# Attention mix on one core: output weights split a round after their loads, fewer single maxima at units' first steps, and the order of the second scores

## The chip, the cores and the metric

The kernel runs on one core of one Trainium2 chip. The metric is device time in microseconds (us). Before the change, three runs took 1511.3 us in the median (1510.62 to 1514.53).

## The reference

Two attention branches over the same input of 2048 positions and 512 features are mixed by a gate for each position. Branch A is a local, dilated attention (32 heads of 16, eight keys, two apart). Branch B is full attention with 32 query heads and one shared key and value head.

```python
g = sigmoid((x * gate_w).sum(-1, keepdims=True))
a = A(x, wqkv, wo_a)      # softmax over 8 keys at distance 0, 2, ..., 14
b = B(x, wq, wk, wv, wo_b)  # softmax(q k^T / 4) v, all 2048 keys, k and v shared by 32 heads
out = g * a + (1 - g) * b
```

All is float32. The weights wq and wk of branch B are drawn eight times as large as the others, so the softmax needs its row maximum.

## The kernel before

**Stages.** Until about 270 us the projections run (`stream` over `lumps`), and with them the first part of the row maxima. Then the main loop runs 512 steps, `s` from 0 to 511, and one more for what is left. A step belongs to unit `u = s // 16` (four heads and 512 queries; 32 units) and key tile `kt = s % 16` (128 keys).

**One step.** It issues, in the order of `order`: the scores of two heads and their exponential (`exp_pair(s, 0)`: two matmuls on the lower and upper 64 rows of the array into bank `eb[0]`, one ScalarE activation over 1024 columns); a pair of row maxima for a later unit (`fill_pair` into `m2`: two matmuls, one VectorE reduction over both); a single maximum (`fill_one` into `m1`: one matmul on one half of the array, one VectorE reduction); the scores and the exponential of the other two heads (`exp_pair(s, 1)`); and the weighted sums of the step before (`weighted(s - 1)`, into `po`). In a unit's first step (`kt == 0`) the sums of the unit just ended are complete: `finish_a` transposes `po` on VectorE (L497) and takes reciprocals.

**The maxima.** Each unit needs 64 halves (one matmul and its maximum each); a pair makes two, a single one. They leave `slots` in a fixed order; a single takes half of a slot, lower rows (`odd` 0) first, and leaves the other in `half`. The planner keeps a clock for each engine (`clk`) and the time at which each bank is free (`free`), from fixed costs: `T_R` 0.23, `T_EXP` 0.92, `T_RED2` 1.14, `T_RED1` 0.61, `T_W` 1.21 us. `fill_ready` issues a pair if `m2` will be free within `M2S` = 0.5 us, a single if `m1` will within `M1S` = 0.3 us. `singles(s)` asks whether pairs alone would be too few for what is to go:

```python
return 2 * max(0, 16 * (NU - 1) - 16 - s) + PER_ROW * max(0, NJ - 4 - outs) < to_go()
```

If a unit's maxima are still missing when its start is near, `pause` issues pairs one after the other on the banks `e0`, `e1` and `m2`, ahead of the step's scores. It is asked for when fewer than two steps are left before the due time (six steps ahead of the unit), for what is missing less 2.8 per step.

**The output.** Three phases (`out_phase`, in units 14, 18 and 25) multiply four rows of tiles by the output weights, and make maxima meanwhile; one begins when branch A is far enough and the lead of the maxima is under `LEAD` = 3 units. The last four rows are made by `spread`, four pairs of matmuls to a step, from the time at which at most nine halves are to go.

**Branch A and the output weights.** Branch A runs on GpSimd, as a list of pieces (`work`), two groups to a round; `run_pool` issues pieces while their planned time is less than 2.5 us ahead. The output weights, eight pieces of 128 x 512, are loaded by SyncE (`wo_load`, L625) into one of two buffers and split into a rounded high part (ScalarE copy, L81) and the rest (GpSimd subtraction, L82). Each round of the first five in the main loop takes two entries of `wos`, and an entry holds the load of one piece and the split of the one before. ScalarE works its instructions in their order, so what stands behind a split waits with it.

Of the kernel before, what the change touches and what calls it, by code (L numbers as in the profile page):

```python
# [19 lines left out]
C = D // P  # L20
# [4 lines left out]
NU = NQB * NHG  # L25
# [23 lines left out]
def gated_mix_kernel(ctx, tc, xt, wa, wk, wq, wo_a, wo_b, out):  # L49
# [20 lines left out]
    def home(v):  # L70

        return (v % NB, v - NB) if v < 2 * NB - 2 else ((v - NB) % (NB - 2), v - NB + 2)
# [11 lines left out]
    clk = {"pe": 0.0, "act": 0.0, "dve": 0.0}  # L84

    def after(eng, ready, dur):
        clk[eng] = max(clk[eng], ready) + dur
        return clk[eng]
# [213 lines left out]
    half = []  # L302
    free = {"m2": 0.0, "m1": 0.0, "e0": 0.0, "e1": 0.0, "po": 0.0}
    tasks, shifted, pm = [], set(), []
# [21 lines left out]
    def to_go():  # L326
        return 2 * len(slots) + len(half)
# [137 lines left out]

    pe, pexp, exped = [], {}, {}

    def exp_pair(s, pr, other=False):
        bank, key = (m2, "m2") if other else (eb[pr], f"e{pr}")
        u, kt = divmod(s, NJ)  # L470
        for odd in range(2):
            b = 64 * odd
            nc.tensor.matmul(bank[:, odd, :], kst[b:b + 64, kt * P:(kt + 1) * P], qst[home(u)[0]][b:b + 64, pr, :], start=True, stop=True)  # L473
        e = px.tile([P, 2, 512], F32, name="pexp", bufs=6)
        nc.scalar.activation(e, bank, AF.Exp, scale=SCALE)  # L475
        free[key] = after("act", after("pe", free[key], T_R) + T_LAT, T_EXP)
        exped[s] = free[key]
        pexp[s, pr] = e
# [50 lines left out]
    def a_load(g, hf):  # L529
        e = wp.tile([P, HALO + NH, AN], F32, name="aext", bufs=2)  # L530
        src = ad[g]
        nc.gpsimd.dma_start(e.rearrange("p r n -> p (r n)"), bass.AP(tensor=src.tensor, offset=src.offset + NH * hf * AN, ap=[[NJ * AN, P], [1, (HALO + NH) * AN]]))
        aext[g] = e
# [33 lines left out]
    def a_sub(g):  # L567
        lgv = alog[g].rearrange("p w j h -> p w (j h)")
        nc.gpsimd.tensor_sub(lgv, lgv, amx.pop(g).unsqueeze(1).to_broadcast([P, W, NH * AG]))
# [10 lines left out]
    def a_add_up(g):  # L580

        lgv = alog[g].rearrange("p w j h -> p w (j h)")
        half = p2[0].tile([P, W // 2, NH * AG], F32, name="half", tag="tr2", bufs=1)
        asum[g] = p2[0].tile([P, NH, AG], F32, name="asum", bufs=2)
        nc.gpsimd.tensor_add(half, lgv[:, 0:4], lgv[:, 4:8])
        nc.gpsimd.tensor_add(half[:, 0:2], half[:, 0:2], half[:, 2:4])
        nc.gpsimd.tensor_add(asum[g].rearrange("p j h -> p (j h)"), half[:, 0], half[:, 1])
# [19 lines left out]
    p2b = []  # L607
# [15 lines left out]
    def wo_load(k, c):  # L623
        wot[k, c] = p2b[0].tile([P, 512], F32, name="os", tag="two", bufs=2)
        nc.sync.dma_start(wot[k, c], (wo_a, wo_b)[k][c * P:(c + 1) * P, :])  # L625

    def wo_split(k, c):
        t = wot.pop((k, c))
        split(woh[k][:, c, :], wol[k][:, c, :], t, nc.gpsimd)
# [219 lines left out]
    later_rows, spread_at, row_left = [], [0.0], [0]  # L849

    def singles(s):

        return 2 * max(0, 16 * (NU - 1) - 16 - s) + PER_ROW * max(0, NJ - 4 - outs) < to_go()
# [86 lines left out]

    wos = []
    kcs = [(k, c) for k in range(2) for c in range(C)]
    for i in range(2 * C + 1):
        wos.append([(wo_load, kcs[i])] if i < 2 * C else [])
        wos[-1] += [(wo_split, kcs[i - 1])] if i else []

    def work():

        def sub(g, hf):
            yield lambda: ("max", g, hf) in done  # L950
            a_sub(g)
            hooks.append((pool + 3000, a_exp, g, ("exp", g, hf)))
            yield 500
            summing.append((g, hf))

        def sums():

            if summing and ("exp",) + summing[0] in done:
                g, hf = summing.pop(0)
                a_add_up(g)  # L960
                hooks.append((pool + 800, a_sum, g, ("sum", g, hf)))
                yield 800

        def values(g, hf):
            while ("sum", g, hf) not in done:
                if summing:
                    yield lambda: ("exp",) + summing[0] in done
                    yield from sums()
                else:
                    yield lambda: ("sum", g, hf) in done  # L970
            yield lambda: g < 8 or p2b
            yield from a_values(g, hf)
            if g == NAG - 1:
                done.add(hf)

        def load(i):
            if i < len(order):
                yield lambda: order[i][0] // GC < ready_gg
                a_load(*order[i])
                yield 600 if i else 6200  # L980

        order = [(g, hf) for hf in range(2) for g in range(NAG)]
        extra, summing = list(wos), []
        yield from load(0)
        yield from load(1)
        for i in range(0, len(order), 2):
            yield from a_scores(*order[i])
            hooks.append((pool + 3500, a_max, order[i][0], ("max",) + order[i]))
            for k, x in enumerate(a_scores(*order[i + 1])):
                yield x  # L990
                if k == 6:
                    yield from sub(*order[i])
                if k == 11:
                    yield from sums()
            hooks.append((pool + 3500, a_max, order[i + 1][0], ("max",) + order[i + 1]))
            for k, x in enumerate(values(*order[i])):
                yield x
                if k == 6:
                    yield from sub(*order[i + 1])
                if k == 11:  # L1000
                    yield from sums()
            yield from load(i + 2)
            yield from values(*order[i + 1])
            yield from load(i + 3)
            for _ in range(2):
                if p2b and extra:
                    for f, a in extra.pop(0):
                        f(*a)
                    yield 1300
        assert not extra  # L1010

    pieces, blocked = [work()], []

    def run_pool():
# [93 lines left out]
    for s in range(NS + 1):  # L1108
        u, kt = divmod(s, NJ)
        if s == 16 * NB + 4:  # L1110
            half_back()
        if len(stacked) < NU and s > 16 * (home(len(stacked))[1] + 1):
            stack(len(stacked))
        if s < NS and kt == 0 and u not in shifted:
            while u not in shifted:
                clk["pe"] += 0.5
                run_tasks()
                if u not in shifted and left.get(u, 1):
                    assert pause(4)
        v = min(x[0][0] for x in (half, slots, [(NU,)]) if x)  # L1120
        need = left.get(v, NF // NU)
        steps = 16 * v - 6 - s
        short = need - 2.8 * max(0, steps) if v < NU else 0
        lead = (NF - to_go()) / 64 - s / 16
        order = (0, "m2", "m1", 1) if s > 1 else (1, "m2", 0, "m1") if s else ()
        k, n = outs // 4, C - (outs >= NJ - 4)
        if outs == NJ - 4:
            if NU - 3 in shaped and to_go() <= 9 and not later_rows and "last" not in done:
                later_rows.append(spread(list(range(outs, NJ)), n))
            if short > 0 and steps < 2:  # L1130
                pause(short)
        elif due or outs < NJ and s and kt == 0 and outs // NH in done and NHG * (k + 1) - 1 in shaped and (lead < LEAD or s >= 16 * (NHG * (k + 2) + 1)):
            if not due:
                prepare(outs, n)
                due.append(n)
            else:
                out_phase(list(range(outs, outs + 4)), due.pop(), kt == 1)
                outs += 4
                order = (0, "m1", 2)
        elif short > 0 and steps < 2:  # L1140
            pause(short)

        for which in order:
            if which == "m2":
                fill_ready("m2", M2S)
            elif which == "m1":
                if not later_rows and singles(s):
                    fill_ready("m1", M1S)
            elif s < NS:
                exp_pair(s, which % 2 or which // 2, which == 2)  # L1150
        spread_some(4)
        if s:
            weighted(s - 1)
            if kt == 0 and s < NS:
                finish_a(u - 1, nc.gpsimd)
        run_tasks()
        run_pool()
# [64 lines left out]
```

## Time and profile before

| | us |
|---|---|
| median of three runs | 1511.3 |
| profiled execution, device time | 1510.97 |
| its span, first to last instruction | 1509.2 |
| TensorE (PE) busy | 1484.5 (98%) |
| ScalarE (ACT) busy | 1280.1 (85%) |
| VectorE (DVE) busy | 1193.7 (79%) |
| GpSimd (POOL) busy | 1021.5 (68%) |

In the rows, a group shows its line, engine, operation, and `out<-in` by the program's names, then the count, the busy time, the mean duration in ns, and the idle time before it with what ended it. PEld is the weight load of TensorE, which overlaps its matmuls (PE). A row of the timeline begins with its start and its length. In a windows row the length, the busy times with counts, TensorE's granted clock (1.00 is full), the DMA share and GB/s follow one another. The tile `pexp` is an exponential, `pe` a bank of scores, `pm` is `m2`, `ps` is `m1`, `mx` holds maxima, `os` a loaded piece of the output weights and `woh` its high part.

### The profile page before, as it was taken

The numbers are of one execution on the slowest core, as the hardware profiler recorded it, in microseconds if no ns is written. First come the engines' busy times: TensorE is split into PE (matmuls) and PEld (weight loads), VectorE is DVE, ScalarE is ACT, GpSimd is POOL, SyncE is SP. The second block draws the span as 40 slices with busy tenths as digits, with TensorE's granted clock in tenths as the row PEclk, the third lists the DMA queues.
The fourth block names the chain that finished last, engine by engine and source line by source line (L and its number), as shares of the span: only waits on it lengthen the run. The fifth ranks groups of instructions, "written<-read, shape, count | busy, mean of one in ns | idle before, by whom it ended". The sixth has DMA issues, their size and how long they took to land.

```text
span 1509.2 us, 29437 instructions
## 1 busy us (share of the span) xinstructions
PE 1484.5 (98%) x11020; PEld 710.6 (47%) x11020; DVE 1193.7 (79%) x1822; ACT 1280.1 (85%) x1660; POOL 1021.5 (68%) x1804
## 2 busy tenths in 40 slices
PE   9999999999989999999999999999999999999998
PEld 6998988433333333333363334633333363333343
DVE  6966666788878888888888888888888888888812
ACT  5468977899979999999988998899989978998975
POOL 7866988787878889888888789888888040111020
PEclk9999999999999999999999999999999999999999
DMA  6744233121120211211202102021120010000000
GB/s 218 216 146 138 78 102 98 33 83 56 49 84 1 83 58 41 69 40 41 69 27 76 48 30 79 30 70 44 37 69 12 12 33 19 2 2 2 1 1 28
DMA packets 44287, 87.75 MB, mean 58 GB/s; under 512 B 9520, under 2 KB 25952, under 8 KB 39920
## 3 DMA queue, kind: packets, MB, share of 16 engines
q1 hardware_dynamic: 37136, 46.89, 10.3%
q0 software_dynamic: 6432, 37.94, 7.5%
q8 instruction: 86, 1.41, 0.4%
q10 hardware_dynamic: 576, 1.05, 0.2%
q14 instruction: 57, 0.47, 0.1%
HBM read 59.02 MB, written 26.30 MB: 57 GB/s over the span
## 4 chain that ended last, share of the span: by engine, by line
PE 88%; ACT 5%; POOL 2%; DVE 2%; issue 2%; DMA 1%; SPq 0%; DVEq 0%; ACTq 0%; POOLq 0%
PE po L483 32%; PE pe L473 25%; PE pm L324 8%; PE pe L1059 6%; PE ps L324 4%; PE pe L740 4%; PE pm L409 2%; ACT pexp L475 2%; ACT dd L419 2%; PE pm L812 1%; PE ps L409 1%; PE po L409 1%; POOL qlo L220 1%; POOL qraw L213 1%; PE pe L183 1%
## 5 line engine op out<-in xcount | busy, mean ns | idle before, releaser
L475 ACT ACTIVATE pexp<-pe 128x1024 f32<-128x1024 f32 x1021 | 989.5, 1022 | 110.0 <-PE pe L473 105.8
L344 DVE TENSOR_REDUCE mx<-pm 128x2 f32<-128x1024 f32 x506 | 618.0, 1221 | 150.0 <-PE pm L324 147.8
L483 PE MATMUL po<-pexp,vst 128*32 128x512 f32 x4096 | 546.5, 605 | 1.1 <-DVE tt L497 0.7
L473 PE MATMUL pe<-qst,kst 64*128 64x512 f32 x1914 | 532.9, 455 | 7.4 <-ACT pexp L475 7.2
L473 PEld LDWEIGHTS pe<-qst,kst 64*128 64x128 f32 x1914 | 219.8, 185 | 414.4 <-ACT pexp L475 404.8
L355 DVE TENSOR_REDUCE mx<-ps 128x1 f32<-128x512 f32 x473 | 321.4, 680 | 4.1 <-PE ps L324 4.1
L324 PE MATMUL pm<-kst,qst 62*128 62x512 f32 x964 | 199.9, 404 | 1.4 <-ACT pexp L475 0.8
L324 PE MATMUL ps<-kst,qst 62*128 62x512 f32 x447 | 189.2, 423 | 0.5 <-DVE mx L355 0.3
L543 POOL TENSOR_TENSOR pr<-aext 128x256 f32<-128x256 f32 x256 | 182.3, 737 | 2.8 <-ACT dd L419 2.6
L603 POOL TENSOR_TENSOR oa<-oa,av 128x256 f32<-128x256 f32 x224 | 164.0, 732 | 15.0
L483 PEld LDWEIGHTS po<-pexp,vst 128*32 128x32 f32 x4096 | 80.9, 108 | 185.6 <-issue 173.1
L600 POOL TENSOR_TENSOR av<-aext,lg 128x256 f32<-128x256 f32 x224 | 139.3, 622 | 12.7
L509 POOL TENSOR_TENSOR rl<-rl,gate_t 128x16 f32<-128x16 f32 x31 | 6.8, 221 | 175.0 <-DVE rl L503 174.9
L324 PEld LDWEIGHTS ps<-kst,qst 62*128 62x128 f32 x447 | 82.4, 184 | 77.0 <-DVE mx L355 74.2
L1059 PE MATMUL pe<-wah,xl 64*128 64x384 f32 (+1 forms) x504 | 107.8, 338 | 0.0
L1059 PE MATMUL pe<-wah,xh 64*128 64x384 f32 (+1 forms) x504 | 107.5, 338 | 0.2 <-ACT gate L253 0.2
L1059 PE MATMUL pe<-wal,xh 64*128 64x384 f32 (+1 forms) x504 | 107.5, 337 | 0.0
L419 ACT ACTIVATE dd<-pm 128x512 f32<-128x512 f32 x164 | 90.8, 610 | 17.8 <-PE pm L409 10.8
L429 DVE CUSTOM_DVE_ANT_0 dd<-ps,dd 128x512 f32<-128x512 f32 x82 | 56.7, 692 | 59.5 <-ACT dd L419 29.0
L324 PEld LDWEIGHTS pm<-kst,qst 62*128 62x128 f32 x964 | 94.7, 188 | 9.5 <-DVE mx L344 4.3
L549 POOL TENSOR_TENSOR tr<-pr 128x512 f32<-128x512 f32 x64 | 81.6, 1275 | 3.7
L549 POOL TENSOR_TENSOR tr<-tr 128x256 f32<-128x256 f32 (+1 forms) x128 | 72.5, 566 | 8.7
(214 smaller groups left out, 1902.6 us busy)
## 6 DMA issues: line engine op xcount, KB each, us to landing
aext<-ad POOLq DMA_DIRECT2D x32, 1056.0 KB, 5.5
ad<-stage SPq DMA_DIRECT2D x32, 384.0 KB
qst<-qd SPq DMA_DIRECT2D x60, 128.0 KB
xraw<-xt SPq DMA_DIRECT2D x16, 256.0 KB
qd<-qhi SPq DMA_DIRECT2D x16, 256.0 KB
qd<-qlo SPq DMA_DIRECT2D x16, 256.0 KB
qst<-qd SPq DMA_DIRECT2D x60, 64.0 KB
qst<-ml SPq DMA_DIRECT2D x216, 2.0 KB
```

Of the source, the lines that this page charges most:

```text
L324: nc.tensor.matmul(dst, qst[home(v)[0]][b:b + 62, pr, t * P:(t + 1) * P], kst[b:b + 62, kc * 512:(kc + 1) * 512], start=True, stop=True)
L344: nc.vector.tensor_reduce(m[:, :, pr, t, kc], dst, AX.X, ALU.max)
L355: nc.vector.tensor_reduce(m[:, odd, pr, t, kc:kc + 1], dst, AX.X, ALU.max)
L419: nc.scalar.activation(dd[0][:, odd], m2[:, odd, :], AF.Abs)
L473: nc.tensor.matmul(bank[:, odd, :], kst[b:b + 64, kt * P:(kt + 1) * P], qst[home(u)[0]][b:b + 64, pr, :], start=True, stop=True)
L475: nc.scalar.activation(e, bank, AF.Exp, scale=SCALE)
L483: nc.tensor.matmul(po[32 * i:32 * i + 32, :], vst[:, kt, :], pexp[s, i // 2][:, i % 2, :], start=(kt == 0), stop=(kt == NJ - 1))
L543: nc.gpsimd.tensor_mul(pr[:, k], q, e[:, o:o + NH, AC:2 * AC])
L549: nc.gpsimd.tensor_add(nx, cur[:, :, 0:n], cur[:, :, n:2 * n])
L600: nc.gpsimd.tensor_mul(av, e[:, o:o + NH, 2 * AC:].rearrange("p j (h d) -> p j h d", d=DH), lg[:, w].unsqueeze(3).to_broadcast([P, NH, AG, ...
L603: nc.gpsimd.tensor_add(ao, ao, av)
L1059: nc.tensor.matmul(front[2 if x == last else x % 2][0][:, b, :n], l[h], r[h], start=(i == 0), stop=(i == 3 * C - 1))
```

## The change

Four edits. The scores of a pair can be issued upper rows first; the second pair of a step does so when the half left in `half` is an upper one, that is, when a single has just used the lower rows. A single is not issued in a unit's first step, except in unit 0's and in the last eight units. A round's entry of `wos` now splits two pieces, those loaded in the round before, and asks for two loads, which the planner issues at 5 us later on its clock. A round takes one entry, charged as 2600 ns of GpSimd, instead of two of 1300.

```diff
-    def exp_pair(s, pr, other=False):
+    def exp_pair(s, pr, other=False, first=0):
...
-        for odd in range(2):
+        for odd in (first, 1 - first):
...
+    def wo_soon(k, c):
+        tasks.append((clk["pe"] + 5.0, wo_load, (k, c)))
...
-    for i in range(2 * C + 1):
-        wos.append([(wo_load, kcs[i])] if i < 2 * C else [])
-        wos[-1] += [(wo_split, kcs[i - 1])] if i else []
+    for i in range(0, 2 * C + 2, 2):
+        wos.append([(wo_split, x) for x in kcs[i - 2:i]] if i else [])
+        wos[-1] += [(wo_soon, x) for x in kcs[i:i + 2]]
...
-            for _ in range(2):
-                if p2b and extra:
-                    for f, a in extra.pop(0):
-                        f(*a)
-                    yield 1300
+            if p2b and extra:
+                for f, a in extra.pop(0):
+                    f(*a)
+                yield 2600
...
+        first = 0
         for which in order:
...
-                if not later_rows and singles(s):
+                if not later_rows and (kt or not s or u >= NU - 8) and singles(s):
+                    first = half[0][4] if half else 0
                     fill_ready("m1", M1S)
             elif s < NS:
-                exp_pair(s, which % 2 or which // 2, which == 2)
+                exp_pair(s, which % 2 or which // 2, which == 2, first)
```

## The prediction

> **What bounds the kernel now.** I read the page first, then the waits, the timeline of the steady loop, the windows around the one long stall, and the counts of the two kinds of maximum.
>
> ```profile
> span 1509.2 us, 29437 instructions
> PE 1484.5 (98%) x11020; PEld 710.6 (47%) x11020; DVE 1193.7 (79%) x1822; ACT 1280.1 (85%) x1660; POOL 1021.5 (68%) x1804
> PE 88%; ACT 5%; POOL 2%; DVE 2%; issue 2%; DMA 1%; SPq 0%; DVEq 0%; ACTq 0%; POOLq 0%
> L475 ACT ACTIVATE pexp<-pe 128x1024 f32<-128x1024 f32 x1021 | 989.5, 1022 | 110.0 <-PE pe L473 105.8
> L344 DVE TENSOR_REDUCE mx<-pm 128x2 f32<-128x1024 f32 x506 | 618.0, 1221 | 150.0 <-PE pm L324 147.8
> ```
>
> TensorE (PE) is busy 98% of the span and holds 88% of the chain that ended last. ScalarE's two exponentials of a step (about 1.0 us each) wait 105.8 us in all for PE, and VectorE's pair reductions 147.8 us. So the loop of 512 steps is paced by PE, with ScalarE close behind. How close shows in a step without a single, read from the weight loads of the scores (a step runs from one such row with an idle time of 0.84 to the next):
>
> ```profile
> 1335.40 0.19 PEld L473 LDWEIGHTS pe<-qst,kst 64*128 64x128 f32 x2 [0.84 <-ACT pexp L475]
> 1337.30 0.19 PEld L473 LDWEIGHTS pe<-qst,kst 64*128 64x128 f32 x2 [0.84 <-ACT pexp L475]
> 1339.48 0.19 PEld L473 LDWEIGHTS pe<-qst,kst 64*128 64x128 f32 x2 [0.84 <-ACT pexp L475]
> 1341.66 0.19 PEld L473 LDWEIGHTS pe<-qst,kst 64*128 64x128 f32 x2 [0.84 <-ACT pexp L475]
> ```
>
> The first step has no single and takes 1.90 us, the next two have one and take 2.18 each.
>
> **Part one, the output weights.**
>
> ```profile
> L81 ACT ACTIVATE woh<-os x8: 629/632/634, 318.6 to 568.6; 128x512 fp32r<-128x512 f32 x8
> ACT woh L81 <- DMA os<-wo_b: 4.4, 1, 4.4
> 446.14 0.63 ACT L81 ACTIVATE woh<-os 128x512 fp32r<-128x512 f32 x1 [4.38 <-DMA os<-wo_b]
> 411.29 0.70 DVE L497 STREAM_TRANSPOSE tt<-po 128x512 f32<-128x512 f32 x1
> 451.74 0.72 DVE L497 STREAM_TRANSPOSE tt<-po 128x512 f32<-128x512 f32 x1 [0.92 <-PE po L483]
> 487.01 0.71 DVE L497 STREAM_TRANSPOSE tt<-po 128x512 f32<-128x512 f32 x1
> 521.41 0.71 DVE L497 STREAM_TRANSPOSE tt<-po 128x512 f32<-128x512 f32 x1
> 447.00:450.00 3.00, 2.27 (x11) 1.45 (x15) 1.00 (x1) 2.78 (x4) 3.00 (x4) 0.50 0.02 5
> 450.00:453.00 3.00, 3.00 (x14) 1.16 (x7) 1.93 (x5) 1.37 (x2) 2.33 (x4) 0.50 0.00 0
> ```
>
> Of the eight splits' copies on ScalarE exactly one waits for its load, 4.38 us; queued behind it are the exponentials, and behind those PE. The transposes (L497) come once a unit: 40.45 us, 35.27 us, and 34.40 for the unit after. So the stall with what follows it costs 40.45 + 35.27 - 2 x 34.40 = 6.9 us, more than the wait, because TensorE's granted clock is 0.50 for some 6 us afterwards (the windows' column after the engines). Changed, each split follows its load by a whole round, some 62 us (the copies lie between 318.6 and 568.6 in four rounds' time), so nothing waits. What is late next is ScalarE itself: two copies of 0.63 us now stand together in four rounds. Such a pair exists already:
>
> ```profile
> 504.06 1.94 ACT L475 ACTIVATE pexp<-pe 128x1024 f32<-128x1024 f32 x2 [0.26 <-PE pe L473]
> 507.99 1.15 ACT L81 ACTIVATE woh<-os 128x512 fp32r<-128x512 f32 x2
> 513.05 1.94 ACT L475 ACTIVATE pexp<-pe 128x1024 f32<-128x1024 f32 x2 [0.26 <-PE pe L473]
> ```
>
> Four steps from 504.06 to 513.05 take 8.99 against 4 x 2.15 (34.40 / 16) = 8.60: 0.4 for a pair. The stalled round becomes such a pair (0.4 stays), the last round gains a second copy (0.2). Part one: -6.9 + 0.4 + 0.2 = **-6.3 us**, between -4.4 (the wait alone) and -6.9. GpSimd's two subtractions of a round stay as they are, charged 2600 ns where they had 2 x 1300. On SyncE's queue the loads come 5 us of planned time later, behind whatever strips of maxima and queries were put there meanwhile; those belong to units well ahead, and the loads have a round to spare. They reuse the buffers of the splits just made, which GpSimd has read by then. Nothing.
>
> **Part two, no single at the first steps of units 1 to 23.** Each unit now issues about 15 singles and skips one at its third step, where VectorE is late from the finishing of the previous unit:
>
> ```profile
> 867.53 0.19 PEld L473 LDWEIGHTS pe<-qst,kst 64*128 64x128 f32 x2 [0.84 <-ACT pexp L475]
> 867.88 0.19 PEld L324 LDWEIGHTS pm<-kst,qst 62*128 62x128 f32 x2 [0.16 <-DVE mx L344]
> 869.54 0.19 PEld L473 LDWEIGHTS pe<-qst,kst 64*128 64x128 f32 x2 [0.84 <-ACT pexp L475]
> 1346.60:1381.00 34.40, 10.21 (x15) 1.00 0.00 1
> 1346.60:1381.00 34.40, 19.56 (x16) 1.00 0.00 1
> 1415.70:1459.00 43.30, 3.41 (x5) 1.00 0.01 1
> 1415.70:1459.00 43.30, 9.74 (x8) 1.00 0.01 1
> ```
>
> (The window rows count the reductions of singles, then of pairs: the first two in unit 28, the last two from the start of unit 30 to its end.) The step with the skip takes 2.01, so one with a single (34.40 - 2.01) / 15 = 2.16. Does the planner put the lost single back at the third step? By its own costs, no. There m2 is what it waits for, and m1 comes free T_RED1 = 0.61 after m2, while PE has moved on by T_R = 0.23: 0.38 late, where M1S allows 0.3. The chain that sets this starts with the finishing of the unit, in both kernels. So the first step is a second skip: 23 x (2.16 - 1.90) = **-6.0 us**, between -3.5 (if the new skip costs 2.01 like the old) and -7.
>
> But the 23 halves (single maxima) remain to be done, and `singles` is true wherever I work it out (a unit makes 15 + 2 x 16 = 47 halves, so at step 464, where the rule's threshold is 32, some 68 are to go), so every place for a single is already taken and nothing later takes them up. They arrive at unit 30. Today 2 x 8 + 5 = 21 halves are left there, and they end at step 488 of 512. Changed, 44 are left. Nine steps (480 to 488) issue three each, but two at the third: 26. At step 489 the rule of `pause` applies (one step before the due time of unit 31): 18 left, less 2.8, is 15.2, so eight pairs are issued in a row on e0, e1 and m2, ahead of the exponentials. Their price is VectorE's:
>
> ```profile
> 1423.46 0.19 PEld L473 LDWEIGHTS pe<-qst,kst 64*128 64x128 f32 x2 [0.84 <-ACT pexp L475]
> 1424.24 1.23 DVE L344 TENSOR_REDUCE mx<-pm 128x2 f32<-128x1024 f32 x1 [0.29 <-PE pm L324]
> 1425.38 0.68 DVE L355 TENSOR_REDUCE mx<-ps 128x1 f32<-128x512 f32 x1
> 1425.66 0.19 PEld L473 LDWEIGHTS pe<-qst,kst 64*128 64x128 f32 x2 [0.84 <-ACT pexp L475]
> ```
>
> The reductions of step 488 end 2.60 after its start (1426.06 - 1423.46); the pairs follow at 1.22 each (the mean of L344), and the seventh frees e0, for which the first scores of step 489 wait: 2.60 + 7 x 1.22 = 11.1, instead of 2.20. That is 8.9 us in which ScalarE has nothing to do and PE little. The other seven of the 23 halves are issued in ordinary steps, four of them as singles in steps 485 to 488, which have none today: 4 x 0.26 = 1.0. Together **+9.9 us**, between +4 (half as many pairs, if the planner finds places) and +14 (three pairs more).
>
> The last four rows of the output, spread four pairs of matmuls to a step, start five steps later as well. What covers that:
>
> ```profile
> L812 PE MATMUL pm<-woh,own x48: 387/393/502, 1434.1 to 1481.7; 64*128 64x512 f32 x48
> L812 PE MATMUL pm<-woh,turned x64: 387/392/396, 1439.6 to 1487.8; 64*128 64x512 f32 x64
> 1486.26 0.30 PEld L473 LDWEIGHTS pe<-qst,kst 64*128 64x128 f32 x4 [0.84 <-ACT pexp L475]
> 1489.09 0.30 PEld L473 LDWEIGHTS pe<-qst,kst 64*128 64x128 f32 x4 [0.84 <-ACT pexp L475]
> 1497.53 0.16 PEld L483 LDWEIGHTS po<-pexp,vst 128*32 128x32 f32 x8 [1.26 <-ACT pexp L475]
> ```
>
> They run from 1434.1 to 1487.8, twenty steps; from 1489.09 to the last weighted sum at 1497.53 there are four steps without them. Those take the delayed rows, and the very last step the rest. With that cover gone, a step's worth costs 2.83 (1486.26 to 1489.09) - 1.90 = 0.9. The output phases that wait for the lead to fall below LEAD may begin a unit earlier (a dozen halves are 0.2 of a unit's 64), with the same work: nothing.
>
> **Part three, the order of the second scores.** A step puts seven matmuls on the two halves of the array: two, two, one, two. The half that has the single runs four, the other three, in either order. Before the change every second single leaves with the half that the next scores begin with, the others with the opposite one, and the two steps of 2.18 above are one of each. So **0**, within 0.01 x some 225 such steps = 2 us either way.
>
> **The sum.** -6.3 - 6.0 + 9.9 + 0 = -2.4 us. The profiled run took 1510.97 (1.8 around its span); less 2.4 it is 1508.6. The median of the three runs is 0.3 higher, so I forecast 1511.3 - 2.4 = **1508.9 us**.
>
> **The rivals.**
>
> *A: the single is moved, not lost.* If m1 is planned to be free in time at the third step, that step gets the single that the first one loses. Then nothing is left over at unit 30, and each unit gains 2.01 - 1.90 = 0.11: 1511.3 - 6.3 - 23 x 0.11 = 1502.5. It needs the 0.38 to shrink below 0.3; what else is charged to PE's plan there could do that, the unchanged chain speaks against it.
>
> *B: the order of the halves counts.* If a single in the half that goes first did cost time, the steps with it would be the longer ones. 0.05 on 225 of them would be 11 us: 1508.9 - 11 = 1498. The equal steps speak against it.
>
> *C: the catch-up ends slower.* One mechanism, at step 489: the halves left there. If VectorE's lateness takes a second single from each of the 23 units (at the fourth step, where m1 is then more than 0.3 late as well), 11.5 more pairs cost 14.0, less 23 x 0.26 = 6.0 saved on the way: +8.0, 1516.9. It decides from about 20 halves more (+7, over the bound below); the 15 singles of unit 28, one skip for its finishing, speak against it. PE's clock would add to it:
>
> ```profile
> 447.73 0.29 PEld L473 LDWEIGHTS pe<-qst,kst 64*128 64x128 f32 x2 [5.22 <-ACT pexp L475]
> 454.57 0.19 PEld L473 LDWEIGHTS pe<-qst,kst 64*128 64x128 f32 x2 [0.84 <-issue]
> SPq L461 <- POOL ml L447: 246.8, 16, 46.8
> ```
>
> After the stall two steps took 6.84 instead of 4.30 at a clock of 0.50: 2.5 us more. In the catch-up PE is not idle but has two matmuls every 1.22 us; whether that keeps the clock, this trace does not show, so 2.5 stands in the range. The Trainium skill (TensorE: Matmul & The Clock Gate, Part 1: The HAM clock gate) says that after an idle window of about 3.4 us the array runs at half its clock until it has been busy for such a window. By that rule, with the sparse pairs counted as idle, the catch-up would cost 12.4 instead of 9.9 and the sum be +0.1; the trace agrees with the rule after the idle 5 us, where it granted 0.50.
>
> *D: the splits still wait.* SyncE's strips wait up to 46.8 us for GpSimd (the last row); loads behind such a wait come late. A wait as long as a round would put the 6.3 back: 1508.9 + 6.3 = 1515.2. Rounds of 62 us speak against it.
>
> **How the numbers follow.** The forecast's case has 0.6, A 0.13, B 0.07, C 0.14, D 0.06. The forecast's own range is 1504 to 1513.5, from the bounds of its terms, the catch-up's above all. A is inside the range that I give, B is left out; above, it reaches to C's middle: 1502 to 1516.5. A run tells a change from none at about 0.3%, 4.5 us: under 1506.8 or over 1515.8. Faster: A and B and a tenth of the forecast's case, 0.26. Slower: most of C, little of D, 0.15. Within: 0.59.
>
> **What would show it.** The wait of L81 for a load is gone, and no stretch at clock 0.50 near 450 us; between transposes 34.1 to 34.2 us where it was 34.4; L355 some 15 to 20 fewer, and in unit 30 a row of eight pair reductions without exponentials beside them, with scores waiting 9 us for VectorE; L812 starting 15 to 20 us later. Wrong would be: singles at third steps (A), steps that shorten by 0.05 all along (B), more than twelve pairs in that row (C), an L81 that still waits (D).

## The result and the profile after

The changed kernel takes 1501.03 us in the median of four runs (1498.46 to 1501.06), the kernel before 1510.96 beside it: a ratio of 0.9925, with 95% between 0.9907 and 0.9944. In a later comparison it was 0.9907 [0.9891, 0.9923]. So the change brings 0.6 to 1.1%. The forecast was 1508.9 with a range from 1502.0; the result lies 1 us below that range, on the side of faster, where most of the chance had been put on no difference that can be told.

The page of the kernel after (profiled execution 1498.46 us):

```profile
span 1496.7 us, 29437 instructions
PE 1477.2 (99%) x11020; PEld 711.1 (48%) x11020; DVE 1192.2 (80%) x1815; ACT 1281.0 (86%) x1664; POOL 1025.9 (69%) x1808
PE 89%; ACT 4%; POOL 3%; issue 2%; DVE 1%; DMA 1%; SPq 0%; DVEq 0%; POOLq 0%; ACTq 0%
L344 DVE TENSOR_REDUCE mx<-pm 128x2 f32<-128x1024 f32 x512 | 625.0, 1221 | 145.5 <-PE pm L324 142.2
L355 DVE TENSOR_REDUCE mx<-ps 128x1 f32<-128x512 f32 x455 | 309.4, 680 | 3.2 <-PE ps L324 3.2
```

PE bounds the kernel as before. The pair reductions (L344) went from 506 to 512. The totals don't say where 12.5 us of the span went; for that the span is cut in three at the transposes of line L497, of which one comes at the start of each unit. The group of the thirty that begin units 1 to 30, before and after:

```profile
L497 DVE STREAM_TRANSPOSE tt<-po x30: 705/707/717, 308.1 to 1417.6; 128x512 f32<-128x512 f32 x30
```

```profile
L497 DVE STREAM_TRANSPOSE tt<-po x30: 701/717/720, 307.3 to 1403.1; 128x512 f32<-128x512 f32 x30
```

The first start is called the lead-in, from it to the last start is the way (units 1 to 29), and the rest of the span is the end (units 30 and 31, with the catch-up). Before: 308.1, 1109.5 and 91.6. After: 307.3, 1095.8 and 93.6. So the way is 13.7 us shorter and the end 2.0 longer. All runs cut in this manner:

| kernel | lead-in | way | end | against the kernel before, 95% |
|---|---|---|---|---|
| before | 308.1 | 1109.5 | 91.6 | |
| after | 307.3 | 1095.8 | 93.6 | 0.9925 [0.9907, 0.9944] |
| e1_weights | 310.4 | 1102.7 | 91.9 | 0.997 [0.996, 0.998] |
| e2_order | 313.2 | 1107.9 | 91.5 | 1.0003 [0.9993, 1.0013] |
| e3_singles | 310.0 | 1103.0 | 93.6 | 0.9975 [0.9966, 0.9984] |
| e4_no_order | 309.4 | 1095.6 | 93.6 | 0.9927 [0.9914, 0.9941] |
| e5_all_units | 311.5 | 1093.6 | 97.4 | 0.9934 [0.9922, 0.9947] |
| e6_due_later | 309.1 | 1095.7 | 93.0 | 0.9921 [0.9907, 0.9934] |
| e7_sixth_step | 310.8 | 1098.1 | 92.5 | 0.9929 [0.9915, 0.9942] |
| e8_two_skips | 309.3 | 1093.8 | 105.7 | 0.9997 [0.9988, 1.0006] |
| e9_split_singly | 310.9 | 1095.9 | 93.6 | 0.993 [0.9915, 0.9945] |
| e10_singly_due_later | 310.0 | 1095.8 | 93.0 | 0.9912 [0.9896, 0.9927] |
| e11_all_units_later | 309.4 | 1093.6 | 98.1 | 0.9927 [0.9911, 0.9943] |
| e12_changed_again | 310.9 | 1095.8 | 93.6 | 0.9907 [0.9891, 0.9923] |

The lead-in, which the edits hardly touch, differs by up to 5.9 us from one execution to the next. The way and the end of the same program (after and e12) agree to 0.1 us. Where the stall is still there the way is less steady: the split's wait is 4.4 us in the trace of before, 4.2 in that of e2 and 5.5 in that of e3, and e2's way is 1.6 us shorter than before's with no difference in its ratio. So single terms of a microsecond or two are read from the way and the end of kernels without the stall, and whether a kernel as a whole is faster from the ratios.

Now the prediction's lines. The output weights after: the group of the copies, ScalarE's timeline at the former stall, and the window around it (length, busy times with counts, granted clock, DMA share, GB/s):

```profile
L81 ACT ACTIVATE woh<-os x8: 629/632/636, 377.3 to 559.7; 128x512 fp32r<-128x512 f32 x8
435.94 1.94 ACT L475 ACTIVATE pexp<-pe 128x1024 f32<-128x1024 f32 x2 [0.19 <-PE pe L473]
437.77 1.15 ACT L81 ACTIVATE woh<-os 128x512 fp32r<-128x512 f32 x2
438.81 5.95 ACT L475 ACTIVATE pexp<-pe 128x1024 f32<-128x1024 f32 x6
430.00:450.00 20.00, 19.84 (x141) 7.03 (x141) 16.71 (x19) 18.89 (x22) 18.50 (x31) 1.00 0.31 103
```

The copies stand in pairs and wait for nothing, the exponentials follow without a gap, and the clock stays at 1.00 where it had been 0.50.

The first steps, by the weight loads of the scores at the start of unit 7:

```profile
510.35 0.18 PEld L473 LDWEIGHTS pe<-q,kst 64*128 64x128 f32 x2 [0.84 <-ACT pexp L475]
512.25 0.19 PEld L473 LDWEIGHTS pe<-q,kst 64*128 64x128 f32 x2 [0.84 <-ACT pexp L475]
514.38 0.19 PEld L473 LDWEIGHTS pe<-q,kst 64*128 64x128 f32 x2 [0.84 <-ACT pexp L475]
514.53 0.19 PEld L324 LDWEIGHTS pm<-kst,qst 62*128 62x128 f32 x2
516.27 0.19 PEld L473 LDWEIGHTS pe<-q,kst 64*128 64x128 f32 x2 [0.84 <-ACT pexp L475]
```

The first step takes 1.90, as forecast. The third, still without a single, takes 1.89; it was 2.01 before. Its pair (514.53) follows the scores with no wait for VectorE, where before it waited 0.16 us for the reduction of the pair ahead (at 867.88). That was not forecast.

The end: the reductions of singles, then of pairs, from the start of unit 30 to that of unit 31, and PE's loads, VectorE and the window at the catch-up:

```profile
1401.60:1443.50 41.90, 4.76 (x7) 1.00 0.01 1
1401.60:1443.50 41.90, 14.30 (x12) 1.00 0.01 1
1419.52 0.19 PEld L324 LDWEIGHTS pe<-kst,qst 62*128 62x128 f32 x2 [0.84 <-ACT pexp L475]
1420.13 1.23 DVE L344 TENSOR_REDUCE mx<-pe 128x2 f32<-128x1024 f32 x1 [0.51 <-PE pe L324]
1421.28 1.22 DVE L344 TENSOR_REDUCE mx<-pm 128x2 f32<-128x1024 f32 x1
1421.41 0.30 PEld L473 LDWEIGHTS pe<-qst,kst 64*128 64x128 f32 x4 [1.55 <-DVE mx L344]
1423.66 0.19 PEld L324 LDWEIGHTS pm<-kst,qst 62*128 62x128 f32 x2 [0.84 <-issue]
1417.00:1423.00 6.00, 4.84 (x38) 1.86 (x34) 4.65 (x5) 4.41 (x7) 0.99 (x1) 1.00 0.02 4
```

7 + 2 x 12 = 31 halves were left at unit 30, not 44. At step 489 two pairs stand in a row, not eight; the scores wait 1.55 us for VectorE, the step takes 4.14 us (1419.52 to 1423.66), and the clock stays at 1.00.

### The profile page after: what moved, and what is told of

Read it like the earlier page. It is cut to its first block, busy times and chain, and to the rows that moved or that the text cites. A ratio compares the mean times of both kernels' runs of the same rounds, so it can differ in the third digit from the quotient of the medians.

```text
span 1496.7 us, 29437 instructions
## 1 busy us (share of the span) xinstructions
PE 1477.2 (99%) x11020; PEld 711.1 (48%) x11020; DVE 1192.2 (80%) x1815; ACT 1281.0 (86%) x1664; POOL 1025.9 (69%) x1808
## 4 chain that ended last, share of the span: by engine, by line
PE 89%; ACT 4%; POOL 3%; issue 2%; DVE 1%; DMA 1%; SPq 0%; DVEq 0%; POOLq 0%; ACTq 0%
PE po L483 34%; PE pe L473 25%; PE pm L324 8%; PE pe L1061 6%; PE ps L324 5%; PE pe L743 4%; PE pm L409 2%; PE pm L815 1%; ACT dd L419 1%; PE ps L409 1%; POOL qlo L220 1%; PE po L409 1%; POOL qraw L213 1%; ACT pexp L475 1%; PE pe L183 1%
## 5 line engine op out<-in xcount | busy, mean ns | idle before, releaser
L344 DVE TENSOR_REDUCE mx<-pm 128x2 f32<-128x1024 f32 x512 | 625.0, 1221 | 145.5 <-PE pm L324 142.2
L473 PE MATMUL pe<-qst,kst 64*128 64x512 f32 x1914 | 522.8, 454 | 3.8 <-ACT pexp L475 2.6
L473 PEld LDWEIGHTS pe<-qst,kst 64*128 64x128 f32 x1914 | 214.5, 184 | 417.0 <-ACT pexp L475 406.6
L355 DVE TENSOR_REDUCE mx<-ps 128x1 f32<-128x512 f32 x455 | 309.4, 680 | 3.2 <-PE ps L324 3.2
L324 PE MATMUL ps<-kst,qst 62*128 62x512 f32 x429 | 180.6, 421 | 0.7 <-DVE mx L429 0.4
L324 PEld LDWEIGHTS ps<-kst,qst 62*128 62x128 f32 x429 | 78.8, 184 | 71.6 <-DVE mx L355 66.6
```

The lines of the kernel that those rows point to most:

```text
L324: nc.tensor.matmul(dst, qst[home(v)[0]][b:b + 62, pr, t * P:(t + 1) * P], kst[b:b + 62, kc * 512:(kc + 1) * 512], start=True, stop=True)
L344: nc.vector.tensor_reduce(m[:, :, pr, t, kc], dst, AX.X, ALU.max)
L355: nc.vector.tensor_reduce(m[:, odd, pr, t, kc:kc + 1], dst, AX.X, ALU.max)
```

## The experiments

### One part at a time

Three kernels are the kernel before with one part of the change each. **e1_weights** has the edit of `wos` and `work` alone:

```diff
...
-    for i in range(2 * C + 1):
-        wos.append([(wo_load, kcs[i])] if i < 2 * C else [])
-        wos[-1] += [(wo_split, kcs[i - 1])] if i else []
+    for i in range(0, 2 * C + 2, 2):
+        wos.append([(wo_split, x) for x in kcs[i - 2:i]] if i else [])
+        wos[-1] += [(wo_soon, x) for x in kcs[i:i + 2]]
...
```

> The kernel before with the output weights' edit alone. My theory: the one wait of a split for its load (4.38 us) goes, and with it the half-clock stretch behind it, less about 0.6 for copies standing in pairs: -6.3 us, and no L81 that waits for a load. Rival (the wait only moves, because the loads reach their buffers late behind SyncE's other waits): within 2 us of before, with an L81 that still waits.

```profile
L497 DVE STREAM_TRANSPOSE tt<-po x30: 704/705/707, 310.4 to 1413.1; 128x512 f32<-128x512 f32 x30
```

The way is 1102.7, 6.8 shorter than before, and the end 0.3 longer: -6.5 where -6.3 was forecast. No copy of L81 waits for a load. The ratio of the whole gives less, 4.5 us with 3.0 to 6.0. The -6.5 is from one trace of each kernel and lies just outside that interval; the lead-in, 2.3 us longer in this trace, is in the whole, and the stall of the kernel before is not the same in every run.

**e2_order** has `first` alone:

```diff
...
-        for odd in range(2):
+        for odd in (first, 1 - first):
...
```

> The kernel before with the order of the second scores alone. My theory: seven matmuls on halves of the array, four on the half with the single in either order: 0, within 2 us. Rival (a single in the half that goes first costs time): -11 us, 0.05 on each of some 225 steps; a weaker form of it, -3 us, is what would be left of the whole change's -9.9 after -6.3 for the weights if the singles' edit gave nothing.

The ratio is 1.0003 [0.9993, 1.0013]. The order is worth nothing that can be told, or at most 2 us either way by that interval.

**e3_singles** has the rule on singles alone:

```diff
-                if not later_rows and singles(s):
+                if not later_rows and (kt or not s or u >= NU - 8) and singles(s):
```

> The kernel before with the rule for singles alone. As predicted: -6.0 on the way and +9.9 at unit 30, so +3.9 us. What the changed kernel's trace suggests instead: some -8 on the way (23 first steps at 1.90, and third steps at 1.90 where they were 2.01) and +2 at the end, so -6 us, with about 30 halves left at unit 30's start instead of 44, because units with an even count of singles make a full pair where before a lone half took the pair's bank, and because output phases hold 36 sums instead of 34.

```profile
L497 DVE STREAM_TRANSPOSE tt<-po x30: 699/716/718, 310.0 to 1413.0; 128x512 f32<-128x512 f32 x30
ACT woh L81 <- DMA os<-wo_b: 5.5, 1, 5.5
```

The way is 6.5 shorter than before, although the one wait for a load is now 5.5 us where it was 4.4. The end is 2.0 longer, as in the kernel after: -4.5 in all, where -6 was expected once the trace of the changed kernel was known. So the two effective parts add up: 6.8 + 6.5 = 13.3 of 13.7 on the way, 0.3 + 2.0 at the end.

**e4_no_order** is the kernel after with the order taken out, a second look at it where no stall disturbs it:

```diff
-                    first = half[0][4] if half else 0
+                    first = 0
```

> The changed kernel with the old order of the second scores (lower rows always first). My theory: as the changed kernel, 1501 us, within 2. Rival (the order gives what is missing): 1504 to 1512 us.

The way is 1095.6 against 1095.8, the end the same. The order does nothing.

### Why the skipped single gains on the way

**e7_sixth_step** leaves as many places out, but each unit's sixth step instead of its first:

```diff
-                if not later_rows and (kt or not s or u >= NU - 8) and singles(s):
+                if not later_rows and (kt != 5 or u == 0 or u >= NU - 8) and singles(s):
```

> The changed kernel with the single left out at the sixth step of units 1 to 23 instead of the first. If it counts only that a unit has one single fewer (an even number, so that pairs are kept whole, and 0.26 us less of PE): units 1 to 29 as much shorter as with the first step, but for the third step, which goes back to 2.00 (+2.3 us in all); the lone halves in m2's place stay at two or fewer. If the first step itself is what matters (the finishing of the unit before then meets a free VectorE): the sixth step's gain is eaten elsewhere, and the stretch of units 1 to 29 is some 7 us longer than the changed kernel's, as in the kernel with the weights' edit alone.

The steps of a unit by the loads of the scores (the unit starts at 858.21; the row of its fifth step is left out):

```profile
L497 DVE STREAM_TRANSPOSE tt<-po x30: 704/706/708, 310.8 to 1408.9; 128x512 f32<-128x512 f32 x30
858.21 0.19 PEld L473 LDWEIGHTS pe<-qst,kst 64*128 64x128 f32 x2 [0.84 <-ACT pexp L475]
860.35 0.18 PEld L473 LDWEIGHTS pe<-qst,kst 64*128 64x128 f32 x2 [0.84 <-ACT pexp L475]
862.53 0.19 PEld L473 LDWEIGHTS pe<-qst,kst 64*128 64x128 f32 x2 [0.84 <-ACT pexp L475]
864.52 0.18 PEld L473 LDWEIGHTS pe<-qst,kst 64*128 64x128 f32 x2 [0.84 <-ACT pexp L475]
...
868.82 0.19 PEld L473 LDWEIGHTS pe<-qst,kst 64*128 64x128 f32 x2 [0.84 <-ACT pexp L475]
870.72 0.19 PEld L473 LDWEIGHTS pe<-qst,kst 64*128 64x128 f32 x2 [0.84 <-ACT pexp L475]
```

The sixth step takes 1.90, and the third is back at 1.99. The way is 1098.1: 4.6 less than with the weights alone (1102.7), 2.3 more than after. So of the 6.9 us that the rule on singles gives after the weights, 4.6 come from any single left out in a unit, and 2.3 from its being the first step's. Most of the second number is the third steps': 1.99 against 1.89 in the units shown, some 2 us in the 21 units whose first step lost its single and that hold no output phase. After a first step without a single VectorE has done with the finishing of the unit in time for the third step's pair. One thing expected here didn't come: 6 lone halves still took the pair's bank (units 1 to 29), where two or fewer had been forecast.

### How much may be skipped

**e8_two_skips** leaves out the first and the ninth step, so that the catch-up must come:

```diff
-                if not later_rows and (kt or not s or u >= NU - 8) and singles(s):
+                if not later_rows and (kt not in (0, 8) or u == 0 or u >= NU - 8) and singles(s):
```

> The changed kernel with singles left out at the ninth step as well as the first, units 1 to 23. This is the prediction's rival C on purpose: the halves are really missing now, and the planner issues about ten pairs in a row before unit 31 and three or so before unit 30. At 1.22 us a pair (eleven more than in the changed kernel) that is +13.4, less 22 x 0.26 = 5.7 on the way: +7.7, some 1508.7 us. If PE's clock falls in the catch-up: 2.5 to 5 more. If pairs in a row are cheap (0.23 us of PE each): -3.

The counts of unit 30 as above, then the catch-up: PE, VectorE and ScalarE, and three windows, the first of them around a smaller catch-up before unit 30:

```profile
1401.60:1454.20 52.60, 5.44 (x8) 0.90 0.01 1
1401.60:1454.20 52.60, 23.36 (x20) 0.90 0.01 1
1423.96 0.50 PE L324 MATMUL pe<-kst,qst 62*128 62x512 f32 x2 [0.63 <-DVE mx L344]
1424.95 1.21 DVE L344 TENSOR_REDUCE mx<-pm 128x2 f32<-128x1024 f32 x1
1425.09 0.76 PE L324 MATMUL pe<-kst,qst 62*128 62x512 f32 x2 [0.63 <-DVE mx L344]
1426.09 2.34 DVE L344 TENSOR_REDUCE mx<-pe 128x2 f32<-128x1024 f32 x2
1432.77 1.94 ACT L475 ACTIVATE pexp<-pe 128x1024 f32<-128x1024 f32 x2 [12.59 <-PE pe L473]
1382.00:1388.00 6.00, 3.54 (x25) 1.40 (x23) 4.66 (x5) 2.56 (x3) 0.00 (x0) 1.00 0.00 0
1419.00:1425.00 6.00, 3.28 (x20) 1.04 (x12) 5.82 (x7) 1.17 (x2) 0.00 (x0) 1.00 0.01 4
1425.00:1433.00 8.00, 4.26 (x14) 1.94 (x14) 6.82 (x7) 0.23 (x1) 0.00 (x0) 0.51 0.00 0
```

8 + 2 x 20 = 48 halves were left, and the catch-up that had been forecast for the kernel after is there: ten pairs in a row, 1.14 us apart (1424.95 to 1426.09), the step 15.5 us long, ScalarE without work for 12.59 us. The end is 105.7, 12.1 longer than after, and the whole is back at the time before (0.9997). The way gains only 2.0 more than with one skip, where 5.7 were reckoned: the smaller catch-up, three pairs in a row from 1382.76, falls into unit 29, and two steps there take 4.0 us each (exponentials at 1380.58, 1384.58 and 1388.55) instead of some 2.15, 3.7 in all. Way and end together are 10.1 us longer than after: more than the +7.7, and close to what was expected if PE's clock falls.

**e5_all_units** drops the exemption of the last eight units:

```diff
-                if not later_rows and (kt or not s or u >= NU - 8) and singles(s):
+                if not later_rows and (kt or not s) and singles(s):
```

> The changed kernel without singles at the first steps of the last units either (only unit 0 keeps its own). By the terms as the traces now give them: seven more first steps at 1.90 instead of 2.16, and third steps at 1.90 instead of 2.00: -2.5 us; at step 489 the catch-up grows from two pairs to three pairs and a single: +1.9. So -0.6 against the changed kernel, 1500 us. Rival (the last eight units have to keep them, as the prediction's price of lost halves would have it: 23 lost cost 9.9, so 7 lost cost 3): +0.5 or more.

```profile
1403.60:1449.70 46.10, 5.45 (x8) 0.96 0.01 2
1403.60:1449.70 46.10, 15.67 (x13) 0.96 0.01 2
1427.00:1431.00 4.00, 4.00 (x21) 1.14 (x18) 1.73 (x3) 2.83 (x4) 1.00 (x1) 0.57 0.00 0
```

The way is 2.2 shorter, the end 3.8 longer. Only 8 + 2 x 13 = 34 halves were left, three more than after; but the step of the catch-up takes 7.68 us instead of 4.14, and 4 us at a clock of 0.57 follow. The exemption pays, 1.6 us in way and end together, where -0.6 had been expected of giving it up; the ratios of the two kernels don't tell them apart.

**e6_due_later** lets the maxima be due four steps ahead of a unit instead of six; **e11_all_units_later** does so without the exemption (and with the splits of e9, below):

```diff
-        steps = 16 * v - 6 - s
+        steps = 16 * v - 4 - s
```

> The changed kernel with the due time of a unit's maxima four steps ahead of the unit instead of six. The planner then issues no pairs in a row at step 489; the halves left go into the steps that follow. If a pair of the catch-up costs 1.22 us of VectorE's time with ScalarE idle: -2 us against the changed kernel. If the pairs are hidden (ScalarE's and PE's other work at the start of the last rows is the bound there): within 0.5.

> As e10, without singles at the first steps of the last eight units. With all units and the old due time the way was 1.7 us shorter and the end 3.3 longer, with TensorE's clock at 0.57 after the catch-up (three pairs and a single). If that catch-up with its clock is the whole cost of the last eight units, the later due time takes it away and this run is 1 to 2 us faster than e10. If the missing halves cost the same wherever they are made: the same as e10, or slower.

In e6, without pairs in a row at step 489, the end shrinks by 0.6 us (93.6 to 93.0), so the catch-up of two pairs had cost little. In e11 the end is 98.1: the later due time does not take back what the missing exemption costs, 4.5 us against after. Its trace shows a catch-up after all, two steps later: a single and a pair in a row at 1425.00, PE busy for about half of the four us that follow them, and then four at half clock.

```profile
1426.00:1430.00 4.00, 2.04 (x12) 1.36 (x14) 2.54 (x4) 1.94 (x2) 1.51 (x3) 0.75 0.01 2
1430.00:1434.00 4.00, 4.00 (x20) 1.49 (x18) 0.00 (x0) 0.35 (x1) 2.60 (x6) 0.50 0.05 5
```

### The splits one at a time, and the best version

**e9_split_singly** keeps a split a round behind its load, but puts one in an entry and takes two entries in a round, as before the change; **e10_singly_due_later** adds the later due time:

```diff
-    for i in range(0, 2 * C + 2, 2):
-        wos.append([(wo_split, x) for x in kcs[i - 2:i]] if i else [])
-        wos[-1] += [(wo_soon, x) for x in kcs[i:i + 2]]
+    for i in range(2 * C + 2):
+        wos.append([(wo_split, kcs[i - 2])] if i > 1 else [])
+        wos[-1] += [(wo_soon, kcs[i])] if i < 2 * C else []
...
```

> The changed kernel with one split and one load at a time, two of them a round, each split still a round behind its load. If two copies standing together cost 0.4 us in each of four rounds and copies apart cost 0 to 0.2: -0.4 to -1.6 us against the changed kernel. If the pairs are hidden: 0.

> As e9, and the due time of the maxima four steps ahead of a unit instead of six, so that no pairs stand in a row at step 489. The sum of the two: -0.6 (the end alone) to -2.2 us against the changed kernel; this is the version that could beat both. If the catch-up of two pairs is hidden as the last run of the later due time suggests: the same as e9.

> The changed kernel itself, on the chip of these runs, for comparison: 1501 us, 0.7% under the kernel before.

**e12_changed_again** is the kernel after itself, beside these on the same chip. All three take the same way to 0.1 us, so the 0.4 us that a pair of copies was said to cost more isn't seen. e10 has 1500.41 us and e12 1499.6, with intervals that overlap almost wholly: no version tried can be told to be faster than the kernel after.

## Why the prediction was wrong

**Weights: right.** -6.3 forecast, -6.5 measured by e1 on way and end, -3.0 to -6.0 by its ratio. The mechanism is the one told: the wait is gone, and with it the stretch at half clock.

**First steps: right in the step, short on the neighbour.** The first step fell to 1.90, and 21 of the 26 units without an output phase (all whose first step the rule covers) lost that single. The third step kept its skip, as the planner's costs had said, so rival A, whose 1502.5 us came nearest to the measured time, was not what happened. Missed was that the third step's pair no longer waits, some 2 us.

**The catch-up: the step that failed.** The prediction said that every place for a single is taken and nothing later takes the lost ones up, so that 44 halves arrive at unit 30 and cost +9.9 us. Measured: 31, and +2.0 us. Counting the halves that each step issues in the 26 units, against three at every step, shows which sentence was wrong:

| halves lost, 26 units | at the first step | at the third | at all others |
|---|---|---|---|
| before | 0 | 27 | 18 |
| e1_weights | 0 | 26 | 20 |
| after | 21 | 26 | 9 |

Before, the planner dropped not one fill in each unit but one at the third step and, in two units of three, another somewhere later: the single, or half of the pair. I had looked at units 28 and 30 alone, and unit 28 has none of these. With the first single left out, half of them go. So 21 are lost and 1 + 9 come back; the units with output phases make one more in all, and 10 more are left at unit 30 (21 before, 31 after). From there the rule of `pause` worked as told: 26 halves were reckoned for steps 480 to 488, one fewer came, six were left, and 6 - 2.8 makes two pairs. The traces also show in what form halves came back. A place of the pair goes to a lone half when a single has left one over and the slots have moved on to the next unit (`fill_ready`); such a reduction reads one half of `pm`. The single reductions on the way (308.1 to 1417.6 us before, 307.3 to 1403.1 us after):

```profile
L355 DVE TENSOR_REDUCE mx<-ps 128x1 f32<-128x512 f32 x430 | 292.2, 679 | 0.9 <-PE ps L324 0.9
L355 DVE TENSOR_REDUCE mx<-pm 128x1 f32<-128x512 f32 x5 | 3.5, 692 | 2.4 <-PE pm L324 2.4
```

```profile
L355 DVE TENSOR_REDUCE mx<-ps 128x1 f32<-128x512 f32 x409 | 278.1, 680 | 0.0
L355 DVE TENSOR_REDUCE mx<-pm 128x1 f32<-128x512 f32 x2 | 1.4, 692 | 0.5 <-PE pm L324 0.4
```

| on the way | singles | lone halves in the pair's bank | pairs | sums of the output phases (two halves each) | halves left at unit 30 |
|---|---|---|---|---|---|
| before | 430 | 5 | 457 | 102 | 21 |
| e1_weights | 430 | 10 | 451 | 108 | 16 |
| after | 409 | 2 | 460 | 106 | 31 |
| e7_sixth_step | 413 | 6 | 457 | 108 | 25 |
| e8_two_skips | 389 | 9 | 454 | 110 | 48 |

From before to after that is -21 for the singles, -3 for the lone halves, +6 for the pairs and +8 for the sums, together the ten halves more that are left. So over the way the singles stayed 21 short; what came back came as pairs made whole and in the output phases. Why the drops fall as they do in each kernel stays open: e7 leaves out as many places as the kernel after and keeps 6 lone halves, e8 leaves out more and has 9.

**The price of a catch-up was about right, where there is one.** By the prediction's working, ten pairs in e8 give 2.60 + 9 x 1.22 = 13.6 us from the start of step 488 to the first scores of step 489; it took 14.2 (1417.64 to 1431.88). The question left open there, whether PE keeps its clock with two matmuls per pair, is answered by e8: it does not. The windows show 1.00 for the first 6 us and 0.51 for the next 8, though PE is busy 3.28 and 4.26 us in them. By the Trainium skill (TensorE: Matmul & The Clock Gate, Part 1: The HAM clock gate) the array goes to half its clock after an idle window of about 3.4 us; e8 agrees if sparse pairs count as idle, the reading under which the prediction gave the catch-up 2.5 us more. With the right number of halves that reading changes nothing for the kernel after: two pairs keep the clock at 1.00, and so do the three pairs of e8's smaller catch-up.

**Order: right**, 0 by e2 and e4. Rivals B, C and D fell with e2, with the count of 31, and with e1. The second output phase began in unit 17 instead of 18, as said; whether any time is in that was not measured apart.

The sum by the measured terms: -6.5 for the weights, -6.9 on the way for the singles (4.6 + 2.3), and 93.6 - 91.9 = +1.7 at the end, together -11.7. That is the way and the end of the table, -13.7 + 2.0. The medians differ by 9.9 us in the first comparison and by 12.8 in the last; a spread of that size is seen in the lead-in alone.

## What to carry to other kernels

Where a planner drops work that doesn't fit, count what it drops over all units before pricing what a further drop leaves over: a drop made on purpose can change how many happen anyway. If a skip is needed, put it where the engine that will be late next still has its one-off work to do (here the first step of a unit, 2.3 us better than the sixth). A debt that is paid at the end costs little while two pairs settle it and costs everything gained when ten must, so leave out only as much as the slack takes.

## What the hardware showed that I had not expected

PE can lose its clock without a long pause: in e8 with 3.28 of 6 us busy, the granted clock fell to 0.51 after some 6 us, and one pair of matmuls of 62 rows went from 0.50 to 0.76 us between 1423.96 and 1425.09. With 4.84 of 6 us busy, in the kernel after, it stayed at 1.00. In e8's smaller catch-up, with 3.54 of 6 us busy (1382 to 1388), it also did, so these traces give no share of busy time at which the clock falls; how long the sparse stretch lasts may matter as much, which no run here tells apart.

The same program also differs from run to run before the loop. The projections' window of the kernel after and of e12, its repetition:

```profile
100.00:200.00 100.00, 97.67 (x984) 89.33 (x981) 63.21 (x197) 85.67 (x211) 76.42 (x133) 1.00 0.36 112
```

```profile
100.00:200.00 100.00, 95.33 (x956) 87.27 (x954) 61.66 (x192) 82.99 (x206) 75.35 (x132) 0.99 0.36 112
```

PE got through 984 matmuls in one and 956 in the other, at clocks of 1.00 and 0.99, and the loop began 3.6 us later. What starts this is not known; in these two traces it is the whole difference of the spans (1496.7 and 1500.3).
